# The 64-row last chunk of eight key tiles as concurrent matmul pairs, in two visits of four tiles, in a gated linear-attention and MLP kernel

## Chip, cores, metric

One core of a Trainium2 chip. The metric is the time of one execution on the device, in microseconds; medians of several runs are given. In the profiles PE is TensorE's matmuls, PEld its weight loads, ACT is ScalarE, DVE VectorE and POOL GpSimd.

## The reference, cut to what matters

```python
x = A_x                                  # 2048 tokens x 448, bf16
g = sigmoid((x * gate_w).sum(-1))
q, k, v = x @ wqkv                       # 16 heads of 28
phi_k = [softmax(k @ w_phi), softmax(-(k @ w_phi))]     # phi_q alike
o = (phi_q @ (phi_k^T v)) / (phi_q @ sum(phi_k)) ; a = o @ wo
b = gelu(x @ w1 + b1) @ w2 + b2          # 448 -> 1792 -> 448
out = g * a + (1 - g) * b
```

The kernel folds `w_phi` into the key and query weights (`Wpk`, `Wpq`). A key tile is 128 tokens; its matmul contracts over 448 inputs, which is three chunks of 128 and one of 64.

## The kernel before

I call a stretch in which TensorE makes the keys or values of a few tiles a visit, the PSUM buffer in which the matmuls of two tiles add up an accumulator, and the time from the start of one matmul to the start of the next a slot. There are four accumulators of two PSUM banks each. Keys of tiles 0 to 7 are made two tiles at a time, with the fourth chunk as a full 128-row matmul of which 64 rows are zero. The values of tiles 4 to 7 (`v_both`) already have the paired form.

```python
def k_pair(u, b1=False):
    pk = four("pk")                       # one of four accumulators, in turn
    for i in range(2):
        t = 2 * u + i
        for c in range(NC4):              # 4 chunks; rows 0:64 of Wpk[:, 3] are zero
            nc.tensor.matmul(pk[:, i, 0:D], lhsT=xT[:, c, t * P:(t + 1) * P],
                             rhs=Wpk[:, c, :], start=(c == 0), stop=(c == NC4 - 1))
    ...                                   # bias transpose into the last one
    k_exp(u, pk)                          # two exponentials on ScalarE (ACT)

def v_both():                             # tiles 4..7: 12 full matmuls, then two pairs
    ...
    for i in range(2):
        nc.tensor.matmul(vs[0][:, i, 0:D + 1], lhsT=x1o[:, i * P:(i + 1) * P],
                         rhs=WvS[0:HP, 3, :], start=False, stop=True)      # rows 0..63
        nc.tensor.matmul(vs[1][:, i, 0:D + 1], lhsT=xT[HP:P, 3, (6 + i) * P:(7 + i) * P],
                         rhs=WvG[HP:P, 3, :], start=False, stop=True)      # rows 64..127
...
swap_on_pool(WvS, WvG)                    # GpSimd (POOL) copies the weights with their
swap_on_pool(WkS, Wpk)                    # row halves exchanged
nc.gpsimd.tensor_copy(out=x1o, in_=xT[HP:P, 3, 512:1024])
...
k_pair(0); k_pair(1); k_norm(0); k_pair(2); k_norm(1); k_pair(3, b1=True); v_both(); ...
```

Later keys and values (`k_two`, `v_two`, tiles 8 to 15), queries (`q_pair`) and the hidden layer (`m_unit`) run wholly in 64-row pairs, half of them on `xS`, a copy of x with exchanged row halves that a DMA makes.

The softmax here doesn't subtract the row's maximum and nothing guards it: scores larger than these inputs give would overflow.

Of the kernel before, what the change touches and what calls it, by code (L numbers as in the profile page):

```python
# [13 lines left out]
D = 448  # L14
# [3 lines left out]
P = 128  # L18
# [5 lines left out]
NJ = 14  # L24
# [4 lines left out]
HP = 64  # L29
# [6 lines left out]
def kernel(  # L36
# [14 lines left out]
    nc = tc.nc  # L51
# [9 lines left out]
    def pair(name):  # L61
        return ps.tile([P, 2, 512], F32, name=name, tag="pair", bufs=3)

    def wide(name):
        return ps.tile([P, 2, 512], F32, name=name, tag="acc", bufs=1)
# [3 lines left out]
    def four(name):  # L69
        turn[0] += 1  # L70
        return wide(name) if turn[0] % 4 == 0 else pair(name)


    xT = consts.tile([P, NC4, S], BF16, name="xT")
# [6 lines left out]
    oT = consts.tile([P, NC4, S], BF16, name="oT")  # L81
# [4 lines left out]
    ident = consts.tile([P, P], BF16, name="ident")  # L86
    b1T = consts.tile([P, NJ], F32, name="b1T")
# [10 lines left out]
    WvG = attn.tile([P, NC4, D + 1], BF16, name="WvG")  # L98
    WvS = attn.tile([P, NC4, D + 1], BF16, name="WvS")
    WkS = attn.tile([P, NC4, D], BF16, name="WkS")  # L100
    Wpk = attn.tile([P, NC4, D], BF16, name="Wpk")
# [9 lines left out]
    b1c = w2_sb[:, 6, 0:P]  # L111
# [28 lines left out]
    def swap_x(h, part=None):  # L140
        ev = slice(2 * h * 512, 2 * h * 512 + 512)
        od = slice(2 * h * 512 + 512, 2 * h * 512 + 1024)
        if part != "odd":
            nc.sync.dma_start(xS[0:HP, :, h, :], xT[HP:P, :, ev])
        if part != "even":
            nc.sync.dma_start(xS[HP:P, 0:3, h, :], xT[0:HP, 0:3, od])
# [29 lines left out]
                          in_=mask[:, PW:PW + 2, None].to_broadcast([P, 2, DH]))  # L176
    nc.gpsimd.memset(KVbd[:], 0.0)
    for g in range(NG):
        nc.gpsimd.tensor_copy(
            out=KVbd[:, g].rearrange("p s (i w) -> p s i w", i=2)[:, :, :, KW - 2:KW],  # L180
            in_=m4[:, None, :, :].to_broadcast([P, 2, 2, 2]))
# [11 lines left out]
    def copy(on_act, out, in_):  # L193
        if on_act:
            nc.scalar.copy(out=out, in_=in_)
        else:
            nc.vector.tensor_copy(out=out, in_=in_)  # L197

    def v_out(u, v_ps, tiles, on_act=False):
        copy(on_act, vaug[:, 2 * u:2 * u + 2, :, 0:PW],  # L200
             v_ps[:, :, 0:D].rearrange("p i (x d) -> p i x d", x=NPR))
        copy(on_act, lg[:, tiles], v_ps[:, :, D])
# [7 lines left out]
                                 rhs=WvG[:, c, :], start=(c == 0), stop=(c == NC4 - 1))  # L210
        v_out(u, v_ps, slice(2 * u, 2 * u + 2), on_act)

    def v_both():
        vs = [four("v_ps"), four("v_ps")]
        for m in range(2):
            for i in range(2):
                t = 4 + 2 * m + i
                for c in range(3):
                    nc.tensor.matmul(vs[m][:, i, 0:D + 1], lhsT=xT[:, c, t * P:(t + 1) * P],  # L219
                                     rhs=WvG[:, c, :], start=(c == 0), stop=False)  # L220
        for i in range(2):
            nc.tensor.matmul(vs[0][:, i, 0:D + 1], lhsT=x1o[:, i * P:(i + 1) * P],  # L222
                             rhs=WvS[0:HP, 3, :], start=False, stop=True)
            nc.tensor.matmul(vs[1][:, i, 0:D + 1], lhsT=xT[HP:P, 3, (6 + i) * P:(7 + i) * P],
                             rhs=WvG[HP:P, 3, :], start=False, stop=True)
        for m in range(2):
            v_out(2 + m, vs[m], slice(4 + 2 * m, 6 + 2 * m))

    def prep(W_T, out_at, engines):
        for m in range(2):  # L230
# [33 lines left out]
    def k_exp(u, pk):  # L264
        tt = slice(2 * u, 2 * u + 2)
        src = pk[:, :, 0:D].rearrange("p i (x w) -> p i x w", w=PW)
        nc.scalar.activation(out=phik[:, tt, :, 0, 0:PW], in_=src, func=ACT.Exp)  # L267
        nc.scalar.activation(out=phik[:, tt, :, 1, 0:PW], in_=src, func=ACT.Exp, scale=-1.0)  # L268

    def k_norm(u):  # L270
        tt = slice(2 * u, 2 * u + 2)
        sums = work.tile([P, 32, 2], F32, name="sums", bufs=3)
        ph = phik[:, tt].rearrange("p t x s w -> p (t x s) w")[:, :, 0:PW]
        ph = ph.rearrange("p y (h d) -> p y h d", d=DH)
        nc.vector.reduce_sum(out=sums[:], in_=ph, axis=AX.X)  # L275
        rec = work.tile([P, 32, 2], F32, name="rec", bufs=3)
        nc.vector.reciprocal(out=rec[:], in_=sums[:])  # L277
        parts = [(nc.gpsimd, 0, 32)] if u < 7 else [(nc.vector, 0, 16), (nc.gpsimd, 16, 32)]
        for eng, lo, hi in parts:
            eng.tensor_tensor(out=ph[:, lo:hi], in0=ph[:, lo:hi],  # L280
                              in1=rec[:, lo:hi, :, None].to_broadcast([P, hi - lo, 2, DH]),
                              op=ALU.mult)

    def k_pair(u, b1=False):
        pk = four("pk")
        for i in range(2):
            t = 2 * u + i
            for c in range(NC4):
                nc.tensor.matmul(pk[:, i, 0:D], lhsT=xT[:, c, t * P:(t + 1) * P],  # L289
                                 rhs=Wpk[:, c, :], start=(c == 0), stop=(c == NC4 - 1))  # L290
        if b1:
            nc.tensor.matmul(pk[:, 1, 480:480 + NJ], lhsT=b1c, rhs=ident[:, 0:NJ],
                             start=True, stop=True, skip_group_check=True)
        k_exp(u, pk)
        if b1:
            nc.scalar.copy(out=b1T[:], in_=pk[:, 1, 480:480 + NJ])
# [89 lines left out]
    def swap_w(W_S, W):  # L386
        nc.sync.dma_start(W_S[0:HP, :, :], W[HP:P, :, :])
        nc.sync.dma_start(W_S[HP:P, 0:3, :], W[0:HP, 0:3, :])

    def swap_on_pool(W_S, W):  # L390
        nc.gpsimd.tensor_copy(out=W_S[0:HP, :, :], in_=W[HP:P, :, :])
        nc.gpsimd.tensor_copy(out=W_S[HP:P, 0:3, :], in_=W[0:HP, 0:3, :])

    nc.gpsimd.dma_start(b1c[0:NJ, :], B_b1.rearrange("(j p) -> j p", p=P))
    x1o = oT[0:HP, 1, 0:512]
    swap_on_pool(WvS, WvG)
    swap_on_pool(WkS, Wpk)
    nc.gpsimd.tensor_copy(out=x1o, in_=xT[HP:P, 3, 512:1024])
    swap_x(0, "even")
    swap_w(WqS, Wpq)  # L400
    swap_x(0, "odd")
# [8 lines left out]
    nc.sync.dma_start(wo_sb[0:64, 3, :], A_wo[384:448, :])  # L410
    nc.sync.dma_start(wo_sb[64:65, 3, :], B_b2[None, :])

    k_pair(0)
    k_pair(1)
    k_norm(0)
    k_pair(2)
    k_norm(1)
    k_pair(3, b1=True)
    v_both()
    nc.sync.dma_start(w2_sb[:], B_w2.rearrange("(j p) n -> p j n", p=P))  # L420
    k_norm(2)
# [148 lines left out]
```

## Time and profile before

| | before |
|---|---|
| median time | 155.75 us (155.66 to 155.77, 3 runs) |
| span of the profiled execution | 153.4 us, TensorE clock 0.999 |
| TensorE busy | 149.4 us, 97% |
| first key matmul to first value matmul of tiles 4 to 7 | 6.09 us (11.13 to 17.22) |
| first key matmul to the first of the last four output matmuls | 138.94 us (11.13 to 150.07) |

The last two rows are the **key stage** and the **whole path**.

### The profile page before, as it was taken

To read this page: it belongs to the slowest core of one execution; us is meant where nothing else is said; L and a number is where in the kernel's file an instruction comes from. 1 tells how busy PE (TensorE), PEld (TensorE's weight loads), DVE (VectorE), ACT (ScalarE), POOL (GpSimd) and SP (SyncE) were. 2 spreads that over 40 slices of the span, in tenths; PEclk is the share of its full clock that TensorE was granted. 3 is DMA by queue.
4 is the path that set the end of the run, shared out by engine and by line. 5 is a ranking of instruction groups with operands and counts; after the bars stand their busy time and mean duration, and the time that the engine had idled before them with its cause. 6 is when DMAs were issued, how large, how long until landed. Compare 5 with 4: busy or idle time off the path is not lost.

```text
span 153.4 us, 3189 instructions
## 1 busy us (share of the span) xinstructions
PE 149.4 (97%) x1302; PEld 79.8 (52%) x1302; DVE 83.0 (54%) x244; ACT 77.3 (50%) x93; POOL 39.8 (26%) x41
## 2 busy tenths in 40 slices
PE   7999999999999999999999999999999999999992
PEld 2675544444544854444444455555556555555561
DVE  3444989499890050000000059999977999977100
ACT  2569949999889437676777740111311111111112
POOL 7999796949874000000000000000000000000000
PEclk9999999999999999999999999999999999999999
DMA  4996998999990000000000001124332123334411
GB/s 149 235 214 150 215 168 195 231 221 218 232 368 23 4 0 4 0 0 4 0 0 0 4 0 34 34 44 93 94 94 64 41 64 91 74 94 38 109 45 30
DMA packets 27922, 14.11 MB, mean 92 GB/s; under 512 B 19842, under 2 KB 27780, under 8 KB 27908
## 3 DMA queue, kind: packets, MB, share of 16 engines
q1 hardware_dynamic: 26692, 13.25, 38.9%
q10 hardware_dynamic: 1152, 0.65, 1.6%
q8 instruction: 10, 0.16, 0.5%
q14 instruction: 4, 0.03, 0.1%
q0 software_dynamic: 64, 0.01, 0.0%
HBM read 6.11 MB, written 1.84 MB: 52 GB/s over the span
## 4 chain that ended last, share of the span: by engine, by line
PE 97%; ACT 0%; issue 0%; DVE 0%; ACTq 0%
PE y L509 28%; PE hp L450 28%; PE y L515 8%; PE pq L324 8%; PE nm L465 4%; PE pk L289 4%; PE v_ps L308 3%; PE pk L316 3%; PE acc L335 2%; PE v_ps L209 2%; PE warm_ps L371 2%; PE v_ps L219 2%; PE w_ps L236 1%; PE xp L354 1%; PE v_ps L222 0%; ACT res L518 0%
## 5 line engine op out<-in xcount | busy, mean ns | idle before, releaser
L509 PE MATMUL y<-w_sb,gel 128*128 128x448 bf16 (+2 forms) x238 | 45.2, 341 | 0.0
L450 PE MATMUL hp<-xT,w_sb 64*128 64x512 bf16 x196 | 42.6, 376 | 0.0
L450 PE MATMUL hp<-xS,w_sb 64*128 64x512 bf16 x196 | 42.6, 376 | 0.0
L455 ACT ACTIVATE gel<-hp,b1T 128x1024 bf16<-128x1024 f32 x28 | 30.8, 1111 | 13.0 <-PE hp L450 13.0
L518 ACT ACTIVATE res<-y,ungate 128x448 bf16<-128x448 f32 (+2 forms) x17 | 10.4, 612 | 50.3 <-PE y L515 50.1
L509 PEld LDWEIGHTS <-gel 128*128 128x128 bf16 x238 | 22.6, 98 | 19.6
L450 PEld LDWEIGHTS <-w_sb 64*128 64x128 bf16 x392 | 19.0, 94 | 23.0
L280 POOL TENSOR_TENSOR phik<-phik,rec 128x1792 bf16<-128x1792 bf16 (+1 forms) x8 | 24.9, 3128 | 6.5 <-DVE rec L277 6.5
L470 DVE COPY st<-nm 128x32 f32<-128x32 f32 x32 | 4.5, 183 | 35.6 <-PE nm L465 35.6
L486 DVE TENSOR_TENSOR tmp<-nm,al 128x448 bf16<-128x448 f32 x32 | 18.4, 615 | 0.0
L275 DVE TENSOR_REDUCE sums<-phik 128x64 f32<-128x1792 bf16 x8 | 16.0, 2000 | 2.7 <-ACT phik L268 2.7
L515 PE MATMUL y<-wo_sb,oT 128*128 128x448 bf16 (+2 forms) x68 | 14.7, 342 | 0.0
L324 PE MATMUL pq<-xT,Wpq 64*128 64x512 bf16 x56 | 12.9, 376 | 0.0
L324 PE MATMUL pq<-xS,WqS 64*128 64x512 bf16 x56 | 12.9, 376 | 0.0
L329 ACT ACTIVATE EqP<-pq 128x1024 bf16<-128x1024 f32 x8 | 8.4, 1049 | 3.8 <-PE pq L324 3.8
L197 DVE CAST vaug<-v_ps 128x896 bf16<-128x896 f32 x7 | 7.5, 1081 | 4.7 <-PE v_ps L209 2.1
L330 ACT ACTIVATE EqN<-pq 128x1024 bf16<-128x1024 f32 x8 | 8.4, 1052 | 0.0
L465 PE MATMUL nm<-KVbd,EqP 128*128 128x120 bf16 x64 | 8.3, 216 | 0.0
L465 PE MATMUL nm<-KVbd,EqN 128*128 128x120 bf16 x64 | 8.3, 216 | 0.0
L267 ACT ACTIVATE phik<-pk 128x896 bf16<-128x896 f32 x8 | 7.7, 957 | 0.3 <-PE pk L289 0.3
L515 PEld LDWEIGHTS <-oT 128*128 128x128 bf16 x68 | 6.0, 98 | 3.5
L268 ACT ACTIVATE phik<-pk 128x896 bf16<-128x896 f32 x8 | 7.7, 967 | 0.0
(102 smaller groups left out, 160.7 us busy)
## 6 DMA issues: line engine op xcount, KB each, us to landing
w_sb<-in_B_w_dram SPq DMA_DIRECT2D x4, 784.0 KB, 11.4
out_dram<-res SPq DMA_DIRECT2D x15, 112.0 KB, 1.9
w_sb<-in_B_w_dram SPq DMA_DIRECT2D x1, 1568.0 KB, 17.1
xS<-xT SPq DMA_DIRECT2D x2, 256.0 KB
oT<-in_A_x_dram ACTq DMA_DIRECT2D x1, 448.0 KB, 3.2
xS<-xT SPq DMA_DIRECT2D x2, 192.0 KB, 3.0
wo_sb<-in_A_wo_dram SPq DMA_DIRECT2D x1, 336.0 KB
WqS<-Wpq SPq DMA_DIRECT2D x1, 256.0 KB, 3.2
```

The lines of the kernel that those rows point to most:

```text
L275: nc.vector.reduce_sum(out=sums[:], in_=ph, axis=AX.X)
L280: eng.tensor_tensor(out=ph[:, lo:hi], in0=ph[:, lo:hi], in1=rec[:, lo:hi, :, None].to_broadcast([P, hi - lo, 2, DH]), op=ALU.mult)
L324: nc.tensor.matmul(pq[:, i, :], lhsT=w_half(Wpq, WqS, i, k)[:, g * P:(g + 1) * P], rhs=x_half(i, k, h), start=(k == 0), stop=(k == NK - 1))
L329: nc.scalar.activation(out=EqP[:, g, dst], in_=src, func=ACT.Exp)
L330: nc.scalar.activation(out=EqN[:, g, dst], in_=src, func=ACT.Exp, scale=-1.0)
L450: nc.tensor.matmul(hp[:, i, :], lhsT=w1_sb[i * HP:(i + 1) * HP, k, j * P:(j + 1) * P], rhs=x_half(i, k, h), start=(k == 0), stop=(k == NK ...
L455: nc.scalar.activation(out=gel[h][:, j, :], in_=hp[:].rearrange("p a b -> p (a b)"), func=ACT.Gelu_apprx_tanh, bias=b1T[:, j:j + 1])
L465: nc.tensor.matmul(nm[s][:, g * 2 * KW:(g + 1) * 2 * KW], lhsT=E[:, g, tok], rhs=KVbd[:, g, s, :], start=True, stop=True)
L486: nc.vector.tensor_tensor(out=tmp[:, s, :].rearrange("p (x h d) -> p x h d", x=NPR, h=2), in0=nmv[s][:, :, 0:PW].rearrange("p x (h d) -> p ...
L509: nc.tensor.matmul(y, lhsT=gel[t // 8][:, j, (t % 8) * P:(t % 8 + 1) * P], rhs=w2_sb[:, j, cols], start=(j == 0), stop=False)
L515: nc.tensor.matmul(y, lhsT=oT[:, c, tok], rhs=wo_sb[:, c, cols], start=False, stop=(c == NC4 - 1))
L518: nc.scalar.activation(out=res[:, cols], in_=y, func=ACT.Copy, scale=ungate[:, t:t + 1])
```

## The change

Intent: let two 64-row matmuls share the array at once instead of running two 128-row ones with half of their rows zero. `both` is `v_both` made general; keys go through it four tiles at a time; POOL copies the two pieces that the first visit needs ahead of the rest.

```diff
+    def both(name, W, W_S, n, base=4, xo=None, b1=False):
+        xo = x1o if xo is None else xo
+        pair_ps = [four(name), four(name)]
+        if b1:
+            nc.tensor.matmul(pair_ps[1][:, 1, 480:480 + NJ], lhsT=b1c, rhs=ident[:, 0:NJ],
+                             start=True, stop=True)
+        for m in range(2):
+            for i in range(2):
+                t = base + 2 * m + i
+                for c in range(3):
+                    nc.tensor.matmul(pair_ps[m][:, i, 0:n], lhsT=xT[:, c, t * P:(t + 1) * P],
+                                     rhs=W[:, c, :], start=(c == 0), stop=False)
+        for i in range(2):
+            nc.tensor.matmul(pair_ps[0][:, i, 0:n], lhsT=xo[:, i * P:(i + 1) * P],
+                             rhs=W_S[0:HP, 3, :], start=False, stop=True)
+            nc.tensor.matmul(pair_ps[1][:, i, 0:n], lhsT=xT[HP:P, 3, (base + 2 + i) * P:(base + 3 + i) * P],
+                             rhs=W[HP:P, 3, :], start=False, stop=True)
+        return pair_ps
 ...
+    def k_both(base, xo, b1=False):
+        pks = both("pk", Wpk, WkS, D, base, xo, b1)
+        for m, pk in enumerate(pks):
+            k_exp(base // 2 + m, pk)
+        if b1:
+            nc.scalar.copy(out=b1T[:], in_=pks[1][:, 1, 480:480 + NJ])
 ...
     swap_on_pool(WvS, WvG)
-    swap_on_pool(WkS, Wpk)
+    x0o = oT[0:HP, 1, 512:768]
+    nc.gpsimd.tensor_copy(out=x0o, in_=xT[HP:P, 3, 0:256])
+    nc.gpsimd.tensor_copy(out=WkS[0:HP, 3, :], in_=Wpk[HP:P, 3, :])
     nc.gpsimd.tensor_copy(out=x1o, in_=xT[HP:P, 3, 512:1024])
+    nc.gpsimd.tensor_copy(out=WkS[0:HP, 0:3, :], in_=Wpk[HP:P, 0:3, :])
+    nc.gpsimd.tensor_copy(out=WkS[HP:P, 0:3, :], in_=Wpk[0:HP, 0:3, :])
 ...
-    k_pair(0)
-    k_pair(1)
+    k_both(0, x0o)
     k_norm(0)
-    k_pair(2)
+    k_both(4, x1o, b1=True)
     k_norm(1)
-    k_pair(3, b1=True)
     v_both()
```

More of the change, by code (lines that the diff above doesn't have):

```diff
@@ L211, in v_pair, with v_both @@
         v_out(u, v_ps, slice(2 * u, 2 * u + 2), on_act)
-    def v_both():
-        vs = [four("v_ps"), four("v_ps")]
+    def both(name, W, W_S, n, base=4, xo=None, b1=False):
[4 more added lines that the diff above has]
+                             start=True, stop=True)
         for m in range(2):
             for i in range(2):
-                t = 4 + 2 * m + i
+                t = base + 2 * m + i
                 for c in range(3):
-                    nc.tensor.matmul(vs[m][:, i, 0:D + 1], lhsT=xT[:, c, t * P:(t + 1) * P],
-                                     rhs=WvG[:, c, :], start=(c == 0), stop=False)
+                    nc.tensor.matmul(pair_ps[m][:, i, 0:n], lhsT=xT[:, c, t * P:(t + 1) * P],
+                                     rhs=W[:, c, :], start=(c == 0), stop=False)
         for i in range(2):
-            nc.tensor.matmul(vs[0][:, i, 0:D + 1], lhsT=x1o[:, i * P:(i + 1) * P],
-                             rhs=WvS[0:HP, 3, :], start=False, stop=True)
-            nc.tensor.matmul(vs[1][:, i, 0:D + 1], lhsT=xT[HP:P, 3, (6 + i) * P:(7 + i) * P],
-                             rhs=WvG[HP:P, 3, :], start=False, stop=True)
-        for m in range(2):
-            v_out(2 + m, vs[m], slice(4 + 2 * m, 6 + 2 * m))
+            nc.tensor.matmul(pair_ps[0][:, i, 0:n], lhsT=xo[:, i * P:(i + 1) * P],
[3 more added lines that the diff above has]
+        return pair_ps
+    def v_both():
+        for m, v_ps in enumerate(both("v_ps", WvG, WvS, D + 1)):
+            v_out(2 + m, v_ps, slice(4 + 2 * m, 6 + 2 * m))
+    def k_both(base, xo, b1=False):
[4 more added lines that the diff above has]
+            nc.scalar.copy(out=b1T[:], in_=pks[1][:, 1, 480:480 + NJ])
     def prep(W_T, out_at, engines):
```

## The prediction

> **What bounds the kernel now.** I read four views in this order: the page (busy shares, slices, chain), the timeline of TensorE around the four key visits, the timelines of POOL and ACT over the same stretch, and narrow timelines at the places where TensorE goes from 128-row to 64-row matmuls or back.
>
> The page first:
>
> ```profile
> PE 149.4 (97%) x1302; PEld 79.8 (52%) x1302; DVE 83.0 (54%) x244; ACT 77.3 (50%) x93; POOL 39.8 (26%) x41
> PEclk9999999999999999999999999999999999999999
> PE 97%; ACT 0%; issue 0%; DVE 0%; ACTq 0%
> ```
>
> TensorE is busy 97% of the 153.4 us span, its clock is not throttled, and the chain that ends last runs on it for 97%. Nothing else sets the end: TensorE time saved is saved in full, and any hole in TensorE is paid in full. The costly groups further down are the 128-row output matmuls and the 64-row matmuls of the hidden layer, which the change leaves alone; the part it touches, eight key tiles, is small. TensorE's timeline there:
>
> ```profile
> 11.13 6.22 PE L289 MATMUL pk<-Wpk,xT 128*128 128x448 bf16 x32
> 17.19 0.17 PE L292 MATMUL pk<-ident,w_sb 128*128 128x14 bf16 x1
> 17.22 2.46 PE L219 MATMUL v_ps<-WvG,xT 128*128 128x449 bf16 x12
> 19.61 0.36 PE L222 MATMUL v_ps<-WvS,oT 64*128 64x449 bf16 x1
> 19.61 0.36 PE L224 MATMUL v_ps<-WvG,xT 64*128 64x449 bf16 x1
> 19.81 0.35 PE L222 MATMUL v_ps<-WvS,oT 64*128 64x449 bf16 x1
> ```
>
> (Columns: start, length, engine, line, operation.) 32 matmuls start between 11.13 and 17.19: 6.06 / 32 = 0.1894 us each, so no waits are in there. In the value visit that already has the new form, two 64-row matmuls start together at 19.61 and the next two 0.20 later: a pair takes one slot of about 0.19. The single durations (0.35) hold the pipeline's latency and are not what a matmul costs here.
>
> What a change of form costs:
>
> ```profile
> 19.32 0.35 PE L219 MATMUL v_ps<-WvG,xT 128*128 128x449 bf16 x1
> ...
> 50.06 0.38 PE L450 MATMUL hp<-xT,w_sb 64*128 64x512 bf16 x1
> 50.37 0.71 PEld L335 LDWEIGHTS <-phik 128*128 128x128 bf16 x23 [0.42 <-issue]
> 50.37 0.80 PE L335 MATMUL acc<-vaug,phik 128*128 128x58 bf16 x22
> ```
>
> The last full matmul before the pairs starts at 19.32 and the first pair at 19.61: 0.29 instead of 0.19, so 0.10 is lost going from 128 to 64 rows. Going back, 50.06 to 50.37 is 0.31 where the pairs of that group follow one another every 0.2155: again 0.10. In both, the weight loads stop and the trace names no releaser, only issue.
>
> **What the Trainium skill says.** "TensorEngine Tiling (Array Packing)", section Key Properties, says that changing the tiling mode drains the engine while changing the tile within a mode does not. The trace agrees, and gives the size: 0.10 us a change. "TensorE: Matmul & The Clock Gate", section Back-to-back issue gap, puts a warm matmul at N/2.4 + 2.5 ns, 189 ns for 448 columns; the trace shows 189.4. The same page's table in Why this matters for your kernels says that a small-K matmul alone takes as long as a full one and that the gain is concurrency; the common starts at 19.61 agree. "PSUM — Partial Sum Buffer", section Terms, says that a first matmul of a group clears the written bits of its bank but not the data, so the bias transpose that is now put into its bank ahead of the keys stays intact; that is a matter of correctness and no run has shown it yet.
>
> **The change part by part.**
>
> Removed: keys of 448 inputs are three chunks of 128 and one of 64, the last done so far as a full matmul with half its rows zero, eight of them. They become eight 64-row matmuls in four concurrent pairs. Four slots of 0.189 are saved: 0.76 us.
>
> Added: each of the two new visits (four tiles each) goes from 128 to 64 rows and back. The existing value visit's own change stays. Four changes of 0.10: 0.40 us. Net on TensorE without any wait: -0.36 us.
>
> Moved, the half chunks' other copies: a pair needs two tiles' inputs on different row halves, so POOL must have copied the half chunk of x for tiles 0 and 1 (64x256) and the half chunk of the key weights (64x448) into the lower rows before the first pair. POOL was this:
>
> ```profile
> 9.59 1.68 POOL L391 COPY WvS<-WvG 64x1796 bf16<-64x1796 bf16 x1
> 11.31 1.31 POOL L392 COPY WvS<-WvG 64x1347 bf16<-64x1347 bf16 x1
> 12.66 1.68 POOL L391 COPY WkS<-Wpk 64x1792 bf16<-64x1792 bf16 x1
> 14.38 1.30 POOL L392 COPY WkS<-Wpk 64x1344 bf16<-64x1344 bf16 x1
> 15.74 0.61 POOL L398 COPY oT<-xT 64x512 bf16<-64x512 bf16 x1
> ```
>
> POOL is busy without a gap, and the two value-weight copies still come first, to 12.62. From 0.61 for 512 columns and 1.68 for 1796, a copy is about 0.18 + 0.00083 a column. So x's copy (256) takes 0.40, 12.66 to 13.06, and the weights' (448) 0.56, 13.10 to 13.66; with about 0.05 for the signal the first pair can start at 13.72. TensorE wants it at 11.13 + 12 x 0.189 + 0.10 = 13.50. I expect a wait of 0.22 us there, once. For the second visit, the copy of 64x512 now comes next, at 13.70 to 14.31; its data, a transposing load issued at 9.18 that lands at most 4.0 us later by that line's own view, is there by 13.2. TensorE needs it at about 16.6: no wait. The large rest of the key weights' copies (2.6 us) goes to 17.0 and is first needed in the later keys at 26: hidden.
>
> Sum: -0.76 + 0.40 + 0.22 = -0.14 us. The value visit would start at 17.08 instead of 17.22.
>
> **Rivals.**
>
> First, *PSUM buffers and ACT become a wait.* Both buffers of a visit now finish together, so the first exponentials start later:
>
> ```profile
> 12.85 0.92 ACT L267 ACTIVATE phik<-pk 128x896 bf16<-128x896 f32 x1 [0.35 <-PE pk L289]
> 13.66 0.91 ACT L268 ACTIVATE phik<-pk 128x896 bf16<-128x896 f32 x1
> ...
> 19.24 0.25 ACT L296 COPY b1T<-pk 128x14 f32<-128x14 f32 x1
> 21.72 1.02 ACT L329 ACTIVATE EqP<-pq 128x1024 bf16<-128x1024 f32 x1 [2.22 <-PE pq L324]
> ```
>
> The first buffer ends with the second pair, at 13.72 + 0.19 + 0.35 = 14.26, so ACT starts at 14.30 instead of 12.85. Eight exponentials every 0.80 end at 20.7, the bias copy at 20.95. Each accumulator takes the buffer of the fourth accumulator before it: the value visit needs the first keys' exponentials (15.9, wanted at 17.1) and the second's (17.5, wanted at 18.2), the queries the third's (19.1, wanted at 19.8) and the fourth's (20.95, wanted at 21.3). All arrive in time, the tightest by 0.4 us, and ACT has a 2.22 us hole to take the delay. On DVE the two sums-and-reciprocals (5.07 us from 14.61 to 19.68 now) would run from 15.94 to 21.0, so the value copies come 0.8 us later and free the first at 22.2; it is wanted at 22.85. If one of these is worse by half a microsecond, the time is 155.8 to 156.2. The margins speak against it.
>
> Second, *the POOL wait is not there or twice as long.* If the small copies are quicker than the straight line through large ones, the gain is the whole 0.36 (155.4). If POOL is slower, say because a copy of few columns has a larger fixed part or DVE's copies disturb it, the wait grows to 0.4 to 0.6 and the change loses 0.0 to 0.2 (155.8 to 156.0).
>
> Third, *the change of form is dearer.* Two cases are measured, both 0.10 but at other widths, and the first return here leads into a 14-column matmul whose weights must be loaded. At 0.20 a change the four cost 0.80 and eat the whole saving: 155.9 to 156.0.
>
> The later loads (hidden-layer weights, output weights) are issued from a queue whose order does not change, and TensorE shows no wait on them at 42.7; a shift of 0.15 us cannot expose them.
>
> **Range and chances.** The central sum gives 155.75 - 0.14 = 155.6 us. All terms together range from -0.40 (no POOL wait) to about +0.3 (dearer changes or a longer wait); the three runs of before differ by 0.11. I take 155.3 to 156.05. Two per cent is 3.1 us, four times all that the removed matmuls cost, and a loss of that size would need a wait nowhere in sight: faster 0.01, same 0.98, slower 0.01.
>
> **What would show it right or wrong.** In the new profile: the first pair of the first visit starts near 13.7, with TensorE idle some 0.3 before it and POOL's 64x448 copy named; without POOL it would be 13.5. The second visit's pairs start 0.29 after their last full matmul, POOL long done. The four changes sum to 0.40. The value visit starts at 17.0 to 17.1, the first query matmul at 19.8, and everything after runs at the old spacing, shifted by the same amount up to the end. ACT's first exponential starts near 14.3 and its hole before the queries shrinks from 2.2 to about 0.6. Wrong it is if TensorE waits for ACT or DVE before the value or query visits, if the copy of x's second block makes the second pairs wait, or if a shift at 20 us is not kept to the end.

## The result

| | before | after |
|---|---|---|
| median time | 155.70 us (155.43 to 155.83, 6 runs) | 155.36 us (155.17 to 155.51, 6 runs) |
| ratio | | 0.9979, 95% interval 0.9966 to 0.9992 |
| key stage | 6.09 us | 5.73 us |
| whole path | 138.94 us | 138.61 us |
| span of the profiled execution | 153.4 us | 153.5 us |

The result is correct; the bias transpose that is now put into its bank ahead of the keys came through, which the prediction had argued and no run had shown. By the 2% measure the time is "same"; in these runs the interval is clear of 1, a small gain, between 0.1 and 0.5 us. The control below is less clear.

The first thing to learn from the new page is what not to read. The span of the profiled execution did not shrink (153.5 against 153.4), though the last matmuls end earlier. These lines are TensorE's timeline at its end; before:

```profile
150.07 0.36 PE L515 MATMUL y<-wo_sb,oT 128*128 128x112 bf16 x4
```

and after:

```profile
149.80 0.36 PE L531 MATMUL y<-wo_sb,oT 128*128 128x112 bf16 x4
```

TensorE starts its last group 0.27 us sooner. But after the end of ACT's last instruction the span goes on for 2.9 us in the changed kernel (from 150.60) and for 2.5 in the one before (from 150.87); the slowest store of each took 3.2 and 2.7 us to land. One span is one draw of that tail and of the loads at the head. The page of after:

```profile
PE 148.4 (97%) x1302; PEld 78.1 (51%) x1302; DVE 83.1 (54%) x244; ACT 77.2 (50%) x93; POOL 40.0 (26%) x43
PEclk9999999999999999999999999999999999999999
PE 91%; DMA 3%; SPq 2%; issue 0%; DVE 0%; ACT 0%; ACTq 0%
```

The count of matmuls is the same (eight full ones became eight halves). The busy time is 1.0 us less, but that is not the gain, since waits at the head are in the difference too. The clock is full, and the chain begins with a DMA now (SPq is the queue of DMAs that SyncE issues): in this execution the first key matmuls could not start before the query weights' load, which precedes the keys in TensorE's order. That is the head's luck and no effect of the change: the chain of the same kernel's second trace (after_again) has no DMA in it.

TensorE's timeline around the key visits, after:

```profile
11.19 2.44 PE L223 MATMUL pk<-Wpk,xT 128*128 128x448 bf16 x12
13.55 0.36 PE L226 MATMUL pk<-WkS,oT 64*128 64x448 bf16 x1
...
13.75 0.35 PE L226 MATMUL pk<-WkS,oT 64*128 64x448 bf16 x1
...
14.07 2.43 PE L223 MATMUL pk<-Wpk,xT 128*128 128x448 bf16 x12
16.44 0.36 PE L226 MATMUL pk<-WkS,oT 64*128 64x448 bf16 x1
...
16.92 2.47 PE L223 MATMUL v_ps<-WvG,xT 128*128 128x449 bf16 x12
```

The first pair starts 13.55 - 11.19 = 2.36 us after the first key matmul. Twelve full matmuls of 0.189 and one change of form (from 128-row to 64-row matmuls or back) of 0.10 make 2.37: there is no wait. The second visit is the same (16.44 - 14.07 = 2.37), and each return to full matmuls takes 0.28 to 0.29 from the last pair (the first return leads into the small bias matmul at 14.04, which this excerpt leaves out). From first key to first value matmul it is 5.73 us, 0.36 less than before, the whole net saving that was worked out for TensorE.

POOL's timeline, and TensorE's weight loads (PEld) at the two first pairs:

```profile
12.48 0.40 POOL L412 COPY oT<-xT 64x256 bf16<-64x256 bf16 x1
12.82 0.56 POOL L413 COPY WkS<-Wpk 64x448 bf16<-64x448 bf16 x1
13.32 0.62 POOL L414 COPY oT<-xT 64x512 bf16<-64x512 bf16 x1
```

```profile
13.55 0.09 PEld L226 LDWEIGHTS <-oT 64*128 64x128 bf16 x1 [0.37 <-POOL WkS L413]
...
16.43 0.09 PEld L226 LDWEIGHTS <-oT 64*128 64x128 bf16 x1 [0.37 <-issue]
```

The columns of the second fence end with the idle time before the load and its releaser. The weights' copy ended at 13.38 and is named as the releaser in the first visit, but the weight loads had been idle 0.37 us there just as in the second visit, where nothing but issue is named: POOL was done in time and cost nothing. I had expected a wait of 0.22 us here. It is the one term of the sum that this trace doesn't show, and the experiments below say why. So the prediction's own second rival came true here: no POOL wait, a gain of the whole 0.36, and a time of 155.4.

ACT, after:

```profile
14.14 0.92 ACT L281 ACTIVATE phik<-pk 128x896 bf16<-128x896 f32 x1 [1.84 <-PE pk L228]
...
20.53 0.26 ACT L241 COPY b1T<-pk 128x14 f32<-128x14 f32 x1
21.43 1.02 ACT L343 ACTIVATE EqP<-pq 128x1024 bf16<-128x1024 f32 x1 [0.65 <-PE pq L338]
```

The exponentials start 1.3 us later than before and take it out of ACT's hole ahead of the queries, which shrank from 2.22 to 0.65 us. Nothing on TensorE waits for them. After the value visit every stretch is as long as before: from the first query to the first hidden-layer matmul 22.72 us in both, from there to the first attention matmul 46.25 in both, from there to the last output group 61.10 and 61.11. The value visit itself, which now comes right after a pair, takes 2.80 us to the first query instead of 2.78. So 0.33 of the 0.36 us is left in the whole path.

### The profile page after: what moved, and what is told of

It is laid out like the page before. It is cut to its first block, busy times and chain, and to the rows that moved or that the text cites. A ratio compares the mean times of both kernels' runs of the same rounds, so it can differ in the third digit from the quotient of the medians.

```text
span 153.5 us, 3192 instructions
## 1 busy us (share of the span) xinstructions
PE 148.4 (97%) x1302; PEld 78.1 (51%) x1302; DVE 83.1 (54%) x244; ACT 77.2 (50%) x93; POOL 40.0 (26%) x43
## 4 chain that ended last, share of the span: by engine, by line
PE 91%; DMA 3%; SPq 2%; issue 0%; DVE 0%; ACT 0%; ACTq 0%
PE y L525 28%; PE hp L466 28%; PE y L531 8%; PE pq L338 8%; PE nm L481 4%; PE v_ps L322 3%; PE pk L330 3%; DMA WqT<-in_A_wqkv_dram 3%; PE pk L223 3%; PE acc L349 2%; SPq L138 2%; PE v_ps L223 2%; PE w_ps L250 1%; PE pk L226 1%; SPq L126 1%; PE v_ps L226 0%
```

## The experiments

The theory: the gain is four matmul slots (0.76 us) less four changes between 128-row and 64-row matmuls (0.10 each), and TensorE's time is the kernel's time. Rivals: the new order itself brings the gain; the gaps at the changes are waits and not the change's cost; POOL's copies hold up the first visit; ACT or the accumulators are about to bound it. Twelve kernels ran. All gave correct results.

**The control: the changed kernel again (after_again).**

> The changed kernel once more, as the control on the chip of this call. From the first key matmul to the first value matmul its first trace had 5.73 us (before: 6.09). My theory: 0.36 less of TensorE work and no POOL wait, so 5.73 again and about 0.35 us under the kernel before. Rival (a POOL wait that comes and goes with the loads ahead of the keys): up to 0.15 longer in this execution.

Measured: 155.32 us against 155.51 for the kernel before (ratio 0.9993, 0.9978 to 1.0008), key stage 5.83, whole path 138.70. In this execution the first pair was late:

```profile
11.19 2.43 PE L223 MATMUL pk<-Wpk,xT 128*128 128x448 bf16 x12
13.64 0.35 PE L226 MATMUL pk<-WkS,oT 64*128 64x448 bf16 x1
```

That is 2.45 us and not 2.36 from the first key matmul. POOL's chain of copies had started at 9.58 instead of 9.38 (9.59 before), and the key weights were ready at 13.59 instead of 13.38. So the POOL wait exists: here it is 0.09 us, and it was the rival that held and not my theory. The intervals of the two ratios, 0.9979 and 0.9993, overlap, and the second includes 1; the two put the gain in time at 0.33 and 0.11 us, and from runs alone it is no better known than that.

**POOL's copies earlier (pool_early).** TensorE's program is that of the change.

```diff
-    swap_on_pool(WvS, WvG)
 ...
     nc.gpsimd.tensor_copy(out=x0o, in_=xT[HP:P, 3, 0:256])
+    nc.gpsimd.tensor_copy(out=WvS[0:HP, :, :], in_=WvG[HP:P, :, :])
     nc.gpsimd.tensor_copy(out=WkS[0:HP, 3, :], in_=Wpk[HP:P, 3, :])
     nc.gpsimd.tensor_copy(out=x1o, in_=xT[HP:P, 3, 512:1024])
+    nc.gpsimd.tensor_copy(out=WvS[HP:P, 0:3, :], in_=WvG[0:HP, 0:3, :])
```

> The same TensorE program, but POOL copies the half chunks of x and of the key weights about 1.4 us earlier. My theory (there was no POOL wait left in the changed kernel): 5.73 us from first key to first value matmul, first pair 0.28 to 0.29 after the last full matmul, time equal to after_again within 0.1. Rival (a hidden POOL wait): the first pair comes sooner and the stage falls below 5.65.

Measured: 155.25 us (ratio to before 0.9989, 0.9974 to 1.0004), key stage 5.74, whole path 138.62; first pair 2.36 us after the first key matmul. With POOL out of the way by 1.2 us the stage is no shorter than in the first trace of the change, so there the wait was nil, and 5.73 to 5.74 is what TensorE needs.

**Four more changes of form, not one matmul more (extra_switches).** On top of pool_early (cut to the new order):

```diff
+        if name == "pk":
+            for i in range(2):
+                whole(0, i)        # six full matmuls
+                whole(1, i)
+                halves(i)          # one pair
```

> As pool_early, but each key visit pairs its halves in two goes, one after each six full matmuls, so there are four more changes between 128 and 64 rows and not one matmul more. My theory (0.095 us a change): stage 5.73 + 0.38 = 6.11 us, time 0.38 over pool_early, the gain over the kernel before gone. Rival (the drain costs nothing of itself, the gaps were waits): stage and time as pool_early. Rival (0.2 a change): stage 6.5.

Measured: 155.51 us, ratio to before 1.0005 (0.9989 to 1.0020); key stage 6.20, whole path 139.08. Each return from a pair costs about the same as elsewhere, for example:

```profile
12.22 0.36 PE L226 MATMUL pk<-WkS,oT 64*128 64x448 bf16 x1
...
12.52 1.31 PE L222 MATMUL pk<-Wpk,xT 128*128 128x448 bf16 x6
```

0.30 us from pair to full matmul, where a slot is 0.19. The stage grew by 0.46 us for four changes, 0.08 more than I had written down. About 0.03 of it lies before the first pair: six full matmuls and a change make 5 x 0.189 + 0.29 = 1.24 us and the pair starts at 1.27 (10.95 to 12.22). The rest is 0.11 a change. The median time is 0.26 over pool_early's, where 0.38 was expected; runs of one kernel spread as widely as that. The gain over the kernel before is gone, as it should be at some 0.1 us a change. That the changes cost nothing, and that they cost 0.2, are both out.

**Two changes fewer (adjacent).** On top of pool_early, the second visit begins with its pairs, right after those of the first, so that TensorE goes from full to half and back once and not twice; the bias transpose moves to the end of the visit. Cut:

```diff
+        half_first = name == "pk" and base == 4
+        if half_first:
+            for i in range(2):
+                halves(i)          # start=True here, the full ones accumulate after
         for m in range(2):
             for i in range(2):
                 whole(m, i)
+        if not half_first:
+            for i in range(2):
+                halves(i)
```

> As pool_early, but the second key visit starts with its halves, right after those of the first, so two of the changes between 64 and 128 rows go. My theory: stage 5.73 - 0.19 = 5.54 us, time 0.19 under pool_early and about 0.55 under the kernel before, provided that the copy of x's second block is there by 13.9; if the load behind it lands late, a wait of up to 0.3 takes the gain. Rival (changes cost nothing): no difference from pool_early.

Measured: 154.98 us, ratio to before 0.9972 (0.9955 to 0.9990); key stage 5.54, whole path 138.41. The eight halves run as four pairs at 13.73, 13.93, 14.12 and 14.31:

```profile
14.31 0.35 PE L226 MATMUL pk<-WkS,oT 64*128 64x448 bf16 x1
...
14.59 2.44 PE L221 MATMUL pk<-Wpk,xT 128*128 128x448 bf16 x12
```

The stage is 0.20 us shorter than pool_early's with the same matmuls. The proviso held: x's second block was copied by 13.39, ahead of the 13.9 that was written. Together with the experiment before, the change of form is a cost of its own of 0.10 us, and the order of work can avoid it. What TensorE does in these 0.10 us is not shown: its weight loads stop at every change too (idle for 0.20 to 0.37 us), and no run separates the two.

**The order without the pairs (reorder_only).** Two accumulators open, half chunks last, but as full matmuls with zero rows (cut to the key visits):

```diff
-                                 rhs=W_S[0:HP, 3, :], start=False, stop=True)
+                    nc.tensor.matmul(pair_ps[m][:, i, 0:n], lhsT=xT[:, 3, t * P:(t + 1) * P],
+                                     rhs=W[:, 3, :], start=False, stop=True)
```

> The new order of the key matmuls (two accumulators open, half chunk last), but the half chunk as full 128-row matmuls as before: no pair, no change of form in the key visits. My theory (the gain is the four slots less the four changes): stage 6.09 us as before, ratio to before 1.000, ACT's first exponential as late as in the changed kernel or later and nothing waiting for it. Rival (the new order itself brings the gain, or ACT's later start costs): stage or time differs from before by 0.2 or more.

Measured: 155.64 us, ratio to before 1.0009 (0.9997 to 1.0021); key stage 6.08, whole path 138.96 (before: 6.09 and 138.94). ACT's first exponential starts at 14.23, and the trace names no wait of TensorE's in the visits. The order brings nothing and ACT's later start costs nothing; the pairs bring it all.

**Each visit alone (first_only, second_only).** In the first, tiles 4 to 7 are made as before (`k_pair(2)`, `k_pair(3, b1=True)`); in the second, tiles 0 to 3.

> Only tiles 0 to 3 in pairs, tiles 4 to 7 as before. My theory: two slots less two changes, stage 6.09 - 0.18 = 5.91 us, time 0.18 under before. Rival (POOL's copies hold up the first visit): stage 6.0 or more.

> Only tiles 4 to 7 in pairs, tiles 0 to 3 as before. My theory: stage 5.91 us again, time 0.18 under before, the two halves of the change adding up to 0.36. Rival (only one of the visits gains): this or first_only at 6.09.

Measured: key stage 5.92 and 5.94 us, so -0.17 and -0.15, which add up to 0.32 of the 0.36. But the times did not follow: 155.73 us (ratio 1.0011, 0.9999 to 1.0024) and 155.55 (1.0003, 0.9989 to 1.0018), and the whole paths are 139.05 and 138.95, no better than before. The traces show where one visit's gain went. This is TensorE's first weight load from the swapped second half of x, in first_only:

```profile
26.46 0.10 PEld L330 LDWEIGHTS <-xS 64*128 64x128 bf16 x2 [0.38 <-DMA xS<-xT]
```

The swap was issued at 23.62 and landed some 2.8 us later. One of the two row halves of the array waited for it, and from the first query to the key-value sums (the first `acc` matmul) this execution took 30.64 us where before and after take 30.37. In second_only it took 30.50:

```profile
25.83 0.10 PEld L330 LDWEIGHTS <-xS 64*128 64x128 bf16 x2 [0.24 <-DMA xS<-xT]
```

In the kernel before, the swap was issued at 23.10 and, at the same 2.8 us, landed 0.1 us ahead of the first matmul that uses it, at 26.04. That margin is so thin that a few tenths at either end turn it into a wait. I had written that the later loads, those of the hidden-layer and output weights, could not be exposed by a shift of 0.15 us. In the traces of the change they were not; but this swap, which comes before them, I had left out.

**The first visit alone, with the late swap used later (first_slack).** The later keys take, on the row half that waits, the unswapped chunks first:

```diff
-        for k in range(NK):
-            for i in range(2):
+        for n in range(NK):
+            for i, ks in enumerate(((0, 2, 4, 1, 3, 5, 6), (1, 3, 5, 6, 0, 2, 4))):
+                k = ks[n]
```

> first_only came out at 1.0011 of the kernel before, though its key stage was 0.17 us shorter; its trace lost 0.27 us between the queries and the key-value sums, where the swapped half of x landed late. This is first_only with the later keys using that half last, as in adjacent_slack. My theory (the late swap took the gain): stage 5.92 us, 30.37 us from the first query matmul to the key-value sums, time 0.15 to 0.2 under before, ratio about 0.999. Rival (the swap was one bad execution and the time is lost elsewhere, in the loads ahead of the keys): ratio 1.001 again, with 30.37 us in that stretch.

Measured: 155.49 us, ratio 1.0001 (0.9987 to 1.0014). The stretch after the queries is back at 30.37 us. But the key stage was 6.17, not 5.92, and the whole path 139.03: the first pair waited for POOL, 2.62 us after the first key matmul (11.06 to 13.68), a quarter of a microsecond too late:

```profile
13.68 0.35 PE L226 MATMUL pk<-WkS,oT 64*128 64x448 bf16 x1 [0.18 <-POOL WkS L414]
```

So the expectation failed, by the wait that I had left out of this theory and had put into the prediction. The four traces with POOL's order of the change show the rule; a pair without a wait comes 2.36 us after the first key matmul:

| trace | POOL's first copy | first key matmul | weights ready | first pair | wait |
|---|---|---|---|---|---|
| after | 9.38 | 11.19 | 13.38 | 13.55 | 0.00 |
| first_only | 9.63 | 11.46 | 13.63 | 13.83 | 0.01 |
| after_again | 9.58 | 11.19 | 13.59 | 13.64 | 0.09 |
| first_slack | 9.63 | 11.06 | 13.63 | 13.68 | 0.26 |

In these four the copies are ready 4.00 or 4.01 us after the start of POOL's first one, and a pair that waits starts 0.05 later. The wait is therefore 4.05 - 2.36 = 1.69 us less the lead that POOL's first copy has over the first key matmul. That lead is 1.43 to 1.83 us. Both ends move: POOL's first copy starts at 9.38 to 9.63, the first key matmul at 11.06 to 11.46, and in after and first_only TensorE had waited 0.24 and 0.31 us for the query weights' load.

**POOL late (pool_late, pool_mid).** In pool_late all key weights are copied before x, as in the kernel before; in pool_mid only the larger half of them.

```diff
# pool_mid
     swap_on_pool(WvS, WvG)
+    nc.gpsimd.tensor_copy(out=WkS[0:HP, :, :], in_=Wpk[HP:P, :, :])
     nc.gpsimd.tensor_copy(out=x0o, in_=xT[HP:P, 3, 0:256])
-    nc.gpsimd.tensor_copy(out=WkS[0:HP, 3, :], in_=Wpk[HP:P, 3, :])
```

> The changed kernel with POOL's copies in the order of the kernel before: all key weights first, then x. x's half chunk is copied by about 15.8, so the first pair starts about 2.35 us later than 13.5. My theory (a hole in TensorE here is paid in full): stage 5.73 + 2.35 = 8.1 us, time about 157.7, 2.0 over before. Rival (later slack takes it up): time within 0.5 of before.

> The changed kernel with half of the large key-weight copy ahead of x's half chunk on POOL, so the first pair waits about 1.15 us (pool_late: 2.56). My theory: a short hole is paid once, at full clock: stage 5.73 + 1.15 = 6.9 us, time 1.15 over after_again, about 156.5; the clock falls only after the longer hole of pool_late, where the matmuls after it ran at half speed for some 3 us. Rival (any hole drops the clock): stage 7.5 or more and PEclk below 9 in a slice.

pool_mid: 156.54 us, 1.22 over after_again's 155.32; ratio to before 1.0065. It was run at another time. Key stage 7.13, whole path 140.01, both 1.40 over after. The trace names a hole of 1.32 us before the first pair, the clock stays at 1.00, and the hole is found again at the end in full. It is longer than I had said because TensorE started early here (11.05):

```profile
14.81 0.36 PE L226 MATMUL pk<-WkS,oT 64*128 64x448 bf16 x1 [1.32 <-POOL oT L413]
```

pool_late: four runs of 157.86, 157.98, 159.24 and 159.57 us, with mean clocks of 1.000, 0.998, 0.989 and 0.986 (ratio to before 1.0199, 1.0161 to 1.0237, "unclear" by the 2% measure). They are two groups. The two quicker ones are what was expected (157.7 was written). The profiled one is one of the slower two: key stage 9.70 instead of 8.1. Its busy times in stretches (after the name of each: length, busy TensorE, weight loads, VectorE, ACT, POOL, then the clock, DMA share and GB/s):

```profile
13.50:16.10 2.60, 0.09 (x1) 0.00 (x0) 0.00 (x0) 0.00 (x0) 2.50 (x4) 0.91 0.81 198
16.10:18.90 2.80, 2.75 (x11) 0.92 (x12) 0.03 (x1) 1.79 (x3) 0.55 (x1) 0.50 1.18 202
18.90:19.30 0.40, 0.40 (x3) 0.22 (x2) 0.40 (x1) 0.40 (x1) 0.00 (x0) 0.84 1.37 248
```

A mean clock of 0.91 over 2.60 us is 0.47 us at half speed, and 0.84 over 0.40 us is 0.13, so, taken as one stretch, the clock is at half for 0.47 + 2.80 + 0.13 = 3.4 us, from about 15.6 to 19.0. It fell some 2.0 us into the hole (13.6 to 16.15), half a microsecond before the hole's end. The second visit's twelve full matmuls and change of form take 3.33 us (17.05 to 20.38) instead of 2.37. Some 2.9 us at half clock have work in them, which is 1.45 us lost, the distance between the two groups of runs. So the hole of 1.32 us was paid once, and the one of 2.56 us was paid dearer in two of four runs, if the other slow one, which was not traced, lost its time in the same way, as its mean clock suggests. What sets the two groups apart is not shown. That a hole here is taken up by later slack is out.

**All eight tiles in one visit (one_visit).** Two changes fewer, like adjacent, but with all four accumulators open: 24 full matmuls, then four pairs.

> As pool_early, but all eight key tiles in one visit: two changes of form fewer than the change, at the price that all four accumulators are open and ACT's first exponential starts about 2.2 us later than in the changed kernel. My theory (the buffers' margins of 0.4 to 1.1 us are then used up): the first value matmul waits for the first keys' exponentials, about 7.0 us after the first key matmul instead of 5.74, the second accumulator and the queries wait some 0.6 more; time about 1.9 over pool_early, 157.2. Rival (TensorE's work alone decides): stage 5.54 and a gain of 0.2.

Measured: 157.10 us, ratio 1.0107 (1.0089 to 1.0125); key stage 7.00, whole path 140.50, 1.88 over pool_early. ACT's first exponential starts 5.22 us after the first key matmul (at 16.09) instead of 2.95, and TensorE now waits for ACT:

```profile
17.87 1.31 PE L223 MATMUL v_ps<-WvG,xT 128*128 128x449 bf16 x6 [1.32 <-ACT phik L282]
19.49 1.31 PE L223 MATMUL v_ps<-WvG,xT 128*128 128x449 bf16 x6 [0.31 <-ACT phik L282]
```

So the rival of buffers and ACT is real: four accumulators filled before the first exponential are too many, and two, as in the change and in adjacent, cause no such wait. Three were not tried.

**Both repairs together (adjacent_slack).** adjacent and the order of first_slack.

> As adjacent, and the later keys (two rows of tiles at a time) take the chunks of the swapped second half of x last, so that this swap, which landed 0.1 to 0.2 us ahead of its use in most traces and after it in first_only and second_only, has some 0.7 us more. My theory: stage 5.54 us as in adjacent, from the first query matmul to the key-value sums 30.37 us in every execution, time 0.5 under the kernel before. Rival (the load's margin is of no account): same as adjacent within 0.1, with or without a wait.

Measured: 154.81 us against 155.40, ratio 0.9962 (0.9949 to 0.9974); key stage 5.54, from queries to sums 30.37, whole path 138.41. This is the best version found, some 0.6 us under the kernel before and clearly so. Its five runs lie within 154.73 to 155.09, adjacent's six within 154.69 to 155.46; whether the later use of the swap makes that difference is not settled by so few, since adjacent's own trace had no wait for the swap.

## Why the prediction was right, and where not

The time, 155.36 us, lies in the range, near its lower end, and the direction was right. That alone says little: the range of 155.3 to 156.05 also holds the time of the kernel before. The centre was off, with 0.14 us expected and 0.36 found in the key stage, and that the first trace had no POOL wait was luck: of the four traces that could have one, two did. Step by step:

- *TensorE bounds all, so what is saved there is saved in full.* Right: every stretch after the values kept its length to 0.01 us, and the hole of pool_mid was found again at the end. For a longer hole it said too little: in the trace of pool_late the clock fell, and the hole cost 1.45 us more than its length.
- *Four slots of 0.189 saved, four changes of 0.10 added, -0.36 without waits.* Right in the key stage: 6.09 to 5.73, with reorder_only (6.08) for the pairs and extra_switches and adjacent (0.11 and 0.10 a change) for the changes of form. The doubt that a change might cost 0.2 was unfounded.
- *A POOL wait of 0.22 in the first visit, once.* The term that was mis-sized. The mechanism is there, but it measured 0.00, 0.09, 0.01 and 0.26 us in four traces. Two things were off: the copies' total, which I had put at 1.00 us from start to end by adding them, while in the trace (whose lengths on POOL are rough) a short copy starts before the one ahead of it has ended and the two take 0.90; and, larger, TensorE's start against POOL's, which I took from one trace (1.54 us) as if it were fixed, while it ranges from 1.43 to 1.83. So the sum of -0.14 is one possible execution and -0.36 another.
- *PSUM and ACT give no wait.* Right, with margins as worked out: ACT's first exponential at 14.14 (expected 14.3), the hole at 0.65 (0.6), the value copies on VectorE from 21.00 (21.0). one_visit shows how soon it would have gone wrong.
- *Later loads cannot be exposed.* True of the weights that it named, and incomplete. The swapped second half of x lands 0.1 to 0.2 us before its use, and twice it came after, for 0.27 and 0.13 us. I had looked only at the weights used from 42.7 on. In the two traces of the change it was in time.

What stays open: why first_only and second_only were not faster in most of their runs. Their own traces lost 0.27 and 0.13 to the swap, and first_slack's lost 0.26 to POOL, but only one execution of each was traced, and I can't say how often either happens.

## What to carry to other kernels

Put the price of changing the matmul's shape (here 0.10 us a change) into the sum, and order the work so that the halves of neighbouring groups stand side by side: here that was worth half as much again as the pairing. When TensorE is 97% busy, look at what lands just in time around the part you shorten, and at how far starts move between executions; a gain of tenths is then often a race between two queues, which a little slack (an earlier copy, a late load used later) settles. Judge such gains by distances inside the trace from a common event, not by the span.

## What the Trainium skill lacked or had wrong

- "TensorEngine Tiling (Array Packing)", section Key Properties, says that a change of tiling mode drains the engine, but not what it costs. Here a change cost 0.10 to 0.11 us in either direction: two fewer saved 0.20 us, four more cost 0.46, of which some 0.03 was elsewhere. Whether it is the draining that takes this time is not shown.
- "TensorE: Matmul & The Clock Gate", section Why this matters for your kernels, tells to avoid gaps above about 3 us. In the trace of pool_late the clock fell to half some 2.0 us into a gap of 2.56 us and stayed there for 3.4 us, so a shorter gap can do it; two of the four runs had the lower mean clock. The gaps of 1.32 us in the traces of pool_mid and one_visit did not do it.
- "GPSIMD Engine Reference", section Engine selection, calls one-input operations roughly line-rate and gives no duration of a short copy. Here a copy on 64 partitions took 0.40 us for 256 columns, 0.56 for 448 and 1.68 for 1796 by the trace's lengths; the copies that followed the first two started 0.34 and 0.50 us after them.
